# An opening written as a table of 206 steps, and attention products of 32 by 32 for the first three pieces

## The chip, the cores and the metric

The kernel runs on one core of one Trainium2 chip. The metric is device time in microseconds (us) of one execution; the median of several runs stands for a kernel. A trace was taken of one execution of the kernel before.

## The reference

A chunked state space attention (a, B, C and x of 4 batches, 8 heads, 768 steps) gives a matrix of 3072 tokens by 256. Two layers of two products each follow.

```python
# by chunks of 32 steps, per batch and head (la = log a of the chunk)
L = np.exp(cum[:, :, :, None] - cum[:, :, None, :]) * causal
M = np.einsum('bhin,bhjn->bhij', Cc, Bc) * L
y = np.einsum('bhij,bhjd->bhid', M, xc) + np.einsum('bhin,bhnd->bhid', Cc, state) * np.exp(cum)[..., None]
state = decay_full[:, :, None, None] * state + np.sum(Bx, axis=2)
...
h = x @ w_in;   x = np.maximum(0.01 * h, h) @ w_out          # first layer, 256 -> 2048 -> 256
h = np.maximum(x @ w2_in, 0.0);   out = h * h @ w2_out       # second layer
```

## The kernel before, in words

The 3072 tokens are 12 *pieces* of 256, three to a batch. For each piece the attention is made by DVE, ACT and PE, and the first layer then takes blocks of pieces: block 0 is piece 0, block 1 is piece 1, and so on, six blocks of one piece and three of two. The second layer follows by groups of 512 tokens.

*Attention of a piece.* `scan_a` squares the inputs for scales (`squares`; their sums by PE in `powers`), scales and splits every operand in a high and a low fp16 half (`him`/`kmx`, `ch`/`cl`, `xh`/`xl`), and runs two scans over the decays (`lt` and `e1`). Then PE makes S: 32 products, one for each of 16 chunks and half. As four heads lie on four strips of 32 partitions, the weights are block diagonal: `diag` puts the four strips in a cleared 128 by 128 tile (`kbd`, `xbh`, `xbl`, `sbd`), by copies on DVE and ACT for piece 0 and by DMAs for the others. S times the decays is `mk`, split in `mkh` and `mkl`. `scan_b` makes Y of 48 products, scans the states (`stt`), halves and transposes them (`shl`, `t16`), makes Z of 32 products onto Y, and writes `yh` and `yl`, the halves of the first layer's input (for piece 0 a single `y32`).

*Weights* come as 64-bit numbers, 512 KB a chunk, through seven buffers (`wst`). Each of the 16 chunks of the first layer takes two steps on ACT (`split_w`), two on DVE (`split_w1`, to `raw`), and, for the blocks from 1 on, a copy on ACT and a subtraction on DVE (`split_w2`, high and low halves). Block 0 multiplies the raw fp32 weights with `y32`; blocks from 1 on make three products for each one, of halves.

*Order.* The program is written as generators of stages that a planner (`due`, `stages_to`) draws from while blocks are written out; a scheduler then sets the order on each engine, which runs its own in that order. In block 0, `raw_step` writes the weights' steps. `sequence_scales` squares the tiles `all` of one of the later batches.

## Time and profile before

| | |
|---|---|
| median of 3 runs | 605.75 us (605.15 to 606.31) |
| the profiled execution | 606.45 us, its span 604.7 us |
| PE busy | 572.1 us, 95% |
| DVE, ACT busy | 455.6 us, 75%; 445.5 us, 74% |

The span runs from the first to the last instruction on the chip. Times in rows are from its start. An engine's busy share is a mean over stages; matmuls are pipelined, and their ends are modelled, so that one that starts 25 ns after another can be shown as 180 ns long.

### The profile page before, as it was taken

What the parts mean: (1) busy time and instruction counts of PE and PEld (TensorE: products, weight loads), DVE (VectorE), ACT (ScalarE), POOL (GpSimd) and SP (SyncE); (2) the same over time, 40 slices, a digit from 0 to 9 for tenths busy, and PEclk for the clock granted to TensorE, in tenths of its full rate; (3) what the DMA queues carried; (4) which work ended last, traced back from release to release, by engine and by line L of the source; (5) the groups of instructions that cost most, each with busy time, mean ns of one, the idle gap of its engine ahead of it and who ended that gap; (6) DMA issues with size and microseconds to landing.
All of it is one profiled execution on the core that took longest, in us unless ns stands there. A gap on an engine that the chain in (4) does not pass through costs nothing.

```text
span 604.7 us, 11654 instructions
## 1 busy us (share of the span) xinstructions
PE 572.1 (95%) x4610; PEld 516.3 (85%) x4610; DVE 455.6 (75%) x774; ACT 445.5 (74%) x715; POOL 5.2 (1%) x15
## 2 busy tenths in 40 slices
PE   0399999999999999999999999999999999999996
PEld 0388899999999878888888889989999999999996
DVE  6999989569984979567655468787777877877765
ACT  6999876479676868556665588877878777777773
POOL 3000000000000000000000000000000000000000
PEclk9999999999999999999999999999999999999999
DMA  8864845573576663131210000010000100100101
GB/s 295 289 160 129 234 111 116 129 193 92 113 187 189 163 166 36 36 62 46 69 36 0 1 2 0 2 36 1 9 28 1 35 1 2 36 1 0 36 1 35
DMA packets 113574, 46.50 MB, mean 77 GB/s; under 512 B 94448, under 2 KB 103280, under 8 KB 113520
## 3 DMA queue, kind: packets, MB, share of 16 engines
q1 hardware_dynamic: 113520, 45.76, 28.3%
q8 instruction: 36, 0.59, 0.4%
q14 instruction: 18, 0.15, 0.1%
HBM read 36.83 MB, written 3.15 MB: 66 GB/s over the span
## 4 chain that ended last, share of the span: by engine, by line
PE 86%; DVE 7%; ACT 4%; issue 2%; DMA 1%; DVEq 0%; ACTq 0%
PE hp L470 13%; PE hp L471 13%; PE hp L472 13%; PE o L532 4%; PE o L611 4%; PE o L538 4%; PE o L533 4%; PE o L609 4%; PE o L610 4%; PE oo L533 3%; PE oo L538 3%; PE oo L532 3%; PE Ym L611 3%; PE Ym L610 3%; PE Ym L609 3%
## 5 line engine op out<-in xcount | busy, mean ns | idle before, releaser
L509 DVE TENSOR_TENSOR g<-t,g 128x512 fp32r<-128x512 f32 x88 | 60.5, 687 | 52.6 <-ACT t L508 52.4
L587 DVE TENSOR_TENSOR tl<-ts,th 128x1024 fp32r<-128x1024 f32 x48 | 58.8, 1226 | 47.1 <-ACT th L585 47.1
L507 ACT ACTIVATE g<-hp 128x512 fp32r<-128x512 f32 x88 | 52.3, 594 | 47.2 <-PE o L538 33.7
L470 PE MATMUL hp<-yl,w1i 128*128 128x256 f32 (+1 forms) x256 | 83.4, 326 | 0.7 <-DVE yl L449 0.7
L471 PE MATMUL hp<-yh,w1i 128*128 128x256 f32 (+1 forms) x256 | 83.2, 325 | 0.0
L472 PE MATMUL hp<-yh,w1i 128*128 128x256 f32 (+1 forms) x256 | 83.0, 324 | 0.0
L575 ACT ACTIVATE b<-hp 128x512 f32<-128x512 f32 x96 | 57.2, 596 | 33.0 <-PE hp L472 32.8
L470 PE MATMUL hp<-xl,w2i 128*128 128x512 f32 x192 | 75.4, 393 | 0.0
L471 PE MATMUL hp<-xh,w2i 128*128 128x512 f32 x192 | 75.3, 392 | 0.0
L472 PE MATMUL hp<-xh,w2i 128*128 128x512 f32 x192 | 74.8, 389 | 0.0
L585 ACT CAST th<-ts 128x1024 fp32r<-128x1024 f32 x48 | 50.3, 1047 | 16.8 <-DVE ts L584 16.8
L470 PEld LDWEIGHTS hp<-yl,w1i 128*128 128x128 f32 x256 | 48.7, 190 | 4.9 <-DVE yl L449 1.1
L508 ACT ACTIVATE t<-hp 128x512 f32<-128x512 f32 x88 | 52.2, 593 | 0.0
L472 PEld LDWEIGHTS hp<-yh,w1i 128*128 128x128 f32 x256 | 48.7, 190 | 3.7
L471 PEld LDWEIGHTS hp<-yh,w1i 128*128 128x128 f32 x256 | 48.7, 190 | 3.7
L576 ACT ACTIVATE b<-b 128x1024 f32<-128x1024 f32 x48 | 50.9, 1061 | 1.1
L586 DVE TENSOR_TENSOR bl<-b,bh 128x768 fp32r<-128x768 f32 x48 | 45.7, 952 | 0.0
L582 DVE TENSOR_TENSOR ts<-b 128x512 f32<-128x512 f32 x48 | 33.2, 691 | 14.5 <-ACT b L576 13.5
L472 PEld LDWEIGHTS hp<-xh,w2i 128*128 128x128 f32 x192 | 36.1, 188 | 7.8
L470 PEld LDWEIGHTS hp<-xl,w2i 128*128 128x128 f32 x192 | 36.2, 189 | 6.3
L471 PEld LDWEIGHTS hp<-xh,w2i 128*128 128x128 f32 x192 | 36.2, 189 | 5.8
L581 ACT CAST bh<-b 128x768 fp32r<-128x768 f32 x48 | 40.1, 835 | 1.3
(167 smaller groups left out, 1571.4 us busy)
## 6 DMA issues: line engine op xcount, KB each, us to landing
in<-in SPq DMA_DIRECT2D x12, 640.0 KB, 4.9
in<-in SPq DMA_DIRECT2D x12, 512.0 KB, 5.7
all<-in SPq DMA_DIRECT2D x15, 384.0 KB, 4.3
wst<-w1i SPq DMA_DIRECT2D x8, 512.0 KB, 6.6
wst<-w1o SPq DMA_DIRECT2D x8, 512.0 KB, 6.4
wst<-w2i SPq DMA_DIRECT2D x8, 512.0 KB, 7.4
wst<-w2o SPq DMA_DIRECT2D x8, 512.0 KB, 4.2
out_t<-r SPq DMA_DIRECT2D x24, 128.0 KB, 1.7
```

Source lines behind the costliest of these rows:

```text
L470: nc.tensor.matmul(hp, wh[:, k, c], xl[:, :, k], start=(k == 0), stop=False)
L471: nc.tensor.matmul(hp, wh[:, k, c], xh[:, :, k], start=False, stop=False)
L472: nc.tensor.matmul(hp, wl[:, k, c], xh[:, :, k], start=False, stop=(k == KI - 1))
L507: nc.scalar.activation(g[:, 0], hp, AF.Lrelu)
L508: nc.scalar.activation(t, hp, AF.Lrelu)
L509: nc.vector.tensor_tensor(g[:, 1], t, g[:, 0].bitcast(F32), ALU.subtract)
L532: nc.tensor.matmul(self.o[d], wl[:, c], gh, start=(m == 0 and (d == 0 or self.n == 2)), stop=False, **kw)
L575: nc.scalar.activation(b[:, 2 * i : 2 * i + 2], hp.rearrange("p (n t) -> p n t", n=2), AF.Relu)
L576: nc.scalar.activation(b, b, AF.Square)
L585: nc.scalar.copy(th, t)
L586: nc.vector.tensor_tensor(bl, b[:, 1:], bh.bitcast(F32), ALU.subtract)
L587: nc.vector.tensor_tensor(tl, t, th.bitcast(F32), ALU.subtract)
```

## The change

The opening (attention of pieces 0 and 1, first steps of the 16 first-layer chunks, all of block 0 and the high halves for block 1) is no longer drawn by the planner. `ORDER` lists its steps by name, and all queues keep that order (`keep`); the low halves (`f0` to `f15`) end it. The names: `ld` a piece's loads, `l`, `a`, `r`, `e`, `f` a weight chunk's load, ACT steps, DVE steps, high and low half; `in`, `ac`, `ou` a pair of block 0's products in, activation and products out; `c0.` and `c1.` steps of the two pieces. Piece 0's first tile is loaded in two parts. Pieces 0, 1 and 2 make S, Y and Z straight from the strips, by four products of 32 by 32 weights each in place of one of 128 by 128, with no block-diagonal tiles. The planner begins with piece 2, all of whose stages now come behind the opening. Sequence scales of batch 1 are drawn one stage later, ahead of piece 3's `scan_a`.

```diff
+c0.Sl c0.u c0.rb c0.er c0.mt c0.ss a2 c0.kk c0.x3 c0.mk c0.e1 c0.xh c0.mkh c0.xl c0.dec c0.mkl
+c0.Ya a3 c0.ect c0.Yb c0.is c0.qh c0.fa r0 c0.d1 a4 c0.st l7 c0.ql c0.sh a5 c0.sl c0.tr a6 r1
...
+    def keep(ins):
+        if pinned[0]:
+            tc.keep_in_program_order(ins)
+            latest[ins.ins.engine] = ins.ins
+        return ins
...
-    def load_piece(p):
+    def load_piece(p, issue=True):
         v = sp.tile([P, U * (N + T + D)], F32, tag="in1", name="in1", bufs=2)
         w = sp.tile([P, U * 2 * T], F32, tag="in2", name="in2", bufs=2)
-        nc.sync.dma_start(v, in1[p])
-        nc.sync.dma_start(w, in2[p])
+        if issue:
+            keep(nc.sync.dma_start(v, in1[p]))
+            keep(nc.sync.dma_start(w, in2[p]))
+        else:
+            c = U * (N + T)
+            loads[p] = {
+                "b": lambda: keep(nc.sync.dma_start(v[:, :c], in1[p][:, :c]) if p == 0 else nc.sync.dma_start(v, in1[p])),
+                "w": lambda: keep(nc.sync.dma_start(w, in2[p])),
+                "x": lambda: keep(nc.sync.dma_start(v[:, c:], in1[p][:, c:])),
+            }
         return part(v, N + T, D), part(v, 0, N), part(w, T, T), part(v, N, T), part(w, 0, T), part(w, 0, T + N)
...
     def diag(p, dst, src):
+        if p == 2:
+            return src
         for h in range(4):
-            d, v = dst[quad[h], :, h, :], src[quad[h]]
-            if p > 0:
-                nc.sync.dma_start(d, v)
+            nc.sync.dma_start(dst[quad[h], :, h, :], src[quad[h]])
+        return dst
+
+    def product(o, w, m, u, **kw):
+        if len(w.shape) == 4:
+            nc.tensor.matmul(o, w[:, u], m, **kw)
+            return
+        for q in quad:
+            nc.tensor.matmul(o[q], w[q, u], m[q], **kw)
...
+    def opening_piece(p, tiles):
...
+        def M(o, w, m, **kw):
+            for h in quad:
+                keep(nc.tensor.matmul(o[h], w[h], m[h], skip_group_check=True, **kw))
...
+        def s_part(c, first):
+            if first:
+                q["S"] = pz.tile([P, U, T], F32, tag="S", name="S")
+            for u in range(U):
+                M(q["S"][:, u], q["kmx"][:, u], q[c][:, u], start=first and u == 0, stop=not first)
+
+        f["Sh"] = lambda: s_part("ch", True)
+        f["Sl"] = lambda: s_part("cl", False)
...
+        def y_part(*pairs):
+            first = "Y" not in q
+            if first:
+                q["Y"] = pz.tile([P, U, 64], F32, tag="Y", name="Y")
+            for i, (w, m) in enumerate(pairs):
+                for u in range(U):
+                    M(q["Y"][:, u, 0 : T + N], q[w][:, u], q[m][:, u], start=first and i == 0 and u % NC == 0, stop=False)
+
+        f["Ya"] = lambda: y_part(("xh", "mkh"), ("xl", "mkh"))
+        f["Yb"] = lambda: y_part(("xh", "mkl"))
...
+        def z():
+            for m in ("qh", "ql"):
+                for u in range(U):
+                    M(q["Y"][:, u, 0:T], q["t16"][:, u], q[m][:, u], start=False, stop=m == "ql")
...
 
-    loaded = {0: load_piece(0)}
-    for _ in range(W_AHEAD):
-        load_w()
...
     def stage(k):
         a = scan_a(k, loaded.pop(k)) if k < NP else iter(())
-        b = scan_b(k - 1, piece_y(k - 1)) if k > 0 else iter(())
-        bd = sequence_scales(k // NPC + 1) if k % NPC == NPC - 1 and k + 1 < NP else iter(())
+        b = scan_b(k - 1, piece_y(k - 1)) if k > 2 else iter(())
+        at = NPC if k == NPC else 2 * NPC - 1
+        bd = sequence_scales((k + NPC - 1) // NPC) if k > 2 and k % NPC == at % NPC and k + 1 < NP else iter(())
         if k <= APART:
...
             yield
 
-    sc_it = (k for k in range(NP + 1) for _ in stage(k))
-    now = [0, 0]
...
             k = next(sc_it, NP + 1)
             now[:] = (k, now[1] + 1) if k == now[0] else (k, 0)
 
-    stages_to(1)
...
+    def opening():
+        f = {}
+        for p in range(2):
+            f.update({f"c{p}.{n}": v for n, v in opening_piece(p, loaded.pop(p)).items()})
+            f.update({f"ld{p}{n}": v for n, v in loads[p].items()})
+        f["ld2"] = lambda: loaded.update({2: load_piece(2)})
+        for c in range(16):
+            f[f"l{c}"] = load_w
+            f[f"a{c}"] = split_w
+            f[f"r{c}"] = split_w1
+            f[f"e{c}"] = lambda: lows.append(split_w2())
+            f[f"f{c}"] = lambda: lows.pop(0)()
+        for c in range(KO // 2):
+            f[f"in{c}"] = lambda c=c: first.hmm([2 * c, 2 * c + 1])
+            f[f"ac{c}"] = lambda c=c: first.act([2 * c, 2 * c + 1])
+            f[f"ou{c}"] = lambda c=c: products_out(c)
+        pinned[0] = True
+        for n in ORDER:
+            f[n]()
+        while lows:
+            lows.pop(0)()
+        pinned[0] = False
+
+    opening()
+    behind = ExitStack()
+    for ins in latest.values():
```

On PE, where block 0 begins (L439/L440 and the L388 rows are Z of piece 0, `hp` and `oo` block 0's products in and out), before:

```order
L440 LDWEIGHTS sbd
L440 MATMUL Y<-ql,sbd 128x32
L493 MATMUL hp<-y_109,raw 128x256 x12
L526 MATMUL oo<-g_432,raw 128x256 x4
L493 MATMUL hp<-y_109,raw 128x256 x4
L526 MATMUL oo<-g_574,raw 128x256
```

and now:

```order
L388 LDWEIGHTS t_548
L388 MATMUL Y<-ql,t_548 32x32
L714 MATMUL hp<-y_109,raw 128x256 x4
L409 MATMUL S<-mx,ones 128x2
L714 MATMUL hp<-y_109,raw 128x256 x4
L747 MATMUL oo<-g_731,raw 128x256 x4
L714 MATMUL hp<-y_109,raw 128x256 x4
L747 MATMUL oo<-g_758,raw 128x256 x4
L714 MATMUL hp<-y_109,raw 128x256 x4
```

The 128 by 128 weight `sbd` is gone, the strips of the transposed states `t` are loaded instead, and in and out products alternate from the start; piece 1's small products stand among them in groups of 64.

On DVE, from piece 1's `yl` on before (L175 is a low half of a first-layer weight, L413 `ql`, L225 to L227 the clip of piece 3):

```order
L449 SCALAR_TENSOR_TENSOR yl<-Y,fac,yh 128x512
L175 TENSOR_TENSOR w1o<-raw,w1o 128x512
L175 TENSOR_TENSOR w1i<-raw,w1i 128x512
L413 SCALAR_TENSOR_TENSOR ql<-le,sc,qh 128x512
L175 TENSOR_TENSOR w1o<-raw,w1o 128x512
L225 TENSOR_SCALAR d1e<-in_692 128x16
L226 TENSOR_SCALAR in_692<-in_692 128x16x31
L227 MEMSET in_692 128x16
L175 TENSOR_TENSOR w1i<-raw,w1i 128x512
L509 TENSOR_TENSOR g<-t,g 128x512
L175 TENSOR_TENSOR w1o<-raw,w1o 128x512
L175 TENSOR_TENSOR w1i<-raw,w1i 128x512
```

and now, from the last low halves behind that `yl` (L349 to L356 scales of piece 2, L242 to L244 its clip, L247 and L252 its scans):

```order
L197 TENSOR_TENSOR w1o<-raw,w1o 128x512 x3
L768 COPY yf<-oo 128x256
L730 TENSOR_TENSOR g<-t,g 128x512
L349 TENSOR_SCALAR eb<-S 128x3
L242 TENSOR_SCALAR d1e<-in_807 128x16
L243 TENSOR_SCALAR in_807<-in_807 128x16x31
L350 TENSOR_SCALAR eb<-eb 128x3
L244 MEMSET in_807 128x16
L730 TENSOR_TENSOR g<-t,g 128x512
L353 TENSOR_SCALAR sc<-eb 128x3
L354 TENSOR_SCALAR isc<-eb 128x3
L247 SCALAR_TENSOR_TENSOR le<-in_807,delta 128x512
```

Before, the scales, clip and scans of piece 2 stood ahead of piece 1's `yl`, under block 0; now they stand behind it and behind all low halves. Between the `yl` of piece 1 and that of piece 2 there were 45 rows and are 74.

On PE, where block 2 begins (the first row with a new `yl`; S is piece 3's in both, Y piece 3's), before:

```order
L389 LDWEIGHTS kbd_92
L389 MATMUL S_1036<-ch_979,kbd_92 128x32
L390 LDWEIGHTS kbd_92
L390 MATMUL S_1036<-cl_1013,kbd_92 128x32
L470 MATMUL hp_1502<-yl_975,w1i_723 128x256
L471 MATMUL hp_1502<-yh_974,w1i_723 128x256
```

and now:

```order
L370 MATMUL Y_2212<-mkh_2083,xbh_90 128x48
L370 LDWEIGHTS xbh_90
L370 MATMUL Y_2212<-mkl_2084,xbh_90 128x48
L370 LDWEIGHTS xbl_91
L370 MATMUL Y_2212<-mkh_2083,xbl_91 128x48
L689 MATMUL hp_2474<-yl_1977,w1i_711 128x256
L690 MATMUL hp_2474<-yh_1976,w1i_711 128x256
```

Before, S of piece 3 stood ahead of block 2's first product; now S and all of Y of piece 3 do. On ACT, 13 squares of `all` tiles stand ahead of piece 2's `yh`, where there were seven.

## Rows read from the trace of the kernel before

**Rows 1.** The page: busy time, share and instructions of each engine.

```profile
PE 572.1 (95%) x4610; PEld 516.3 (85%) x4610; DVE 455.6 (75%) x774; ACT 445.5 (74%) x715; POOL 5.2 (1%) x15
```

**Rows 2.** Four stretches: length, busy (count) by engine, granted clock, DMA share.

```profile
0.00:29.50 29.50, 5.22 (x116) 4.85 (x116) 24.34 (x69) 23.60 (x48) 5.21 (x15) 1.00 0.82 293
29.50:63.30 33.80, 32.20 (x232) 27.29 (x232) 32.42 (x65) 31.19 (x61) 0.00 (x0) 1.00 0.57 169
63.30:91.60 28.30, 28.29 (x337) 27.76 (x338) 25.01 (x50) 22.07 (x43) 0.00 (x0) 1.00 0.61 145
91.60:604.70 513.10, 506.42 (x3932) 456.38 (x3927) 373.79 (x592) 368.66 (x565) 0.00 (x0) 1.00 0.22 55
```

**Rows 3.** What PE waited for: us in total, times, longest.

```profile
PE S L389 <- ACT kbd L355: 7.6, 1, 7.6
...
PE Y L439 <- DVE er L294: 5.2, 1, 5.2
...
PE o L532 <- DVE yf L547: 1.3, 1, 1.3
```

**Rows 4.** Timeline, start and us: `yl` of pieces 1 and 2, first products behind them.

```profile
62.51 0.75 DVE L449 SCALAR_TENSOR_TENSOR yl<-Y,fac,yh 128x512 fp32r<-128x512 f32 x1
...
63.31 0.39 PE L470 MATMUL hp<-yl,w1i 128*128 128x256 f32 x1 [0.71 <-DVE yl L449]
...
89.92 0.74 DVE L449 SCALAR_TENSOR_TENSOR yl<-Y,fac,yh 128x512 fp32r<-128x512 f32 x1
...
91.63 0.36 PE L470 MATMUL hp<-yl,w1i 128*128 128x256 f32 x1
```

**Rows 5.** Groups by line to 63.3 us; four tiles, two copies each per engine.

```profile
L355 DVE COPY kbd<-kmx 32x512 f16<-32x512 f16 x2 | 0.6, 282 | 0.0
...
L355 ACT COPY kbd<-kmx 32x512 f16<-32x512 f16 x2 | 1.2, 610 | 0.0
```

**Rows 6.** Timeline of PE: first of piece 1's 32 S products, what follows.

```profile
41.45 0.18 PE L389 MATMUL S<-ch,kbd 128*128 128x32 f16 x1
...
42.25 1.54 PE L526 MATMUL oo<-g,raw 128*128 128x256 f32 x6
```

**Rows 7.** Timeline: ACT's and DVE's first instructions on loaded data.

```profile
4.79 0.42 ACT L274 ACTIVATE sq<-in 128x256 bf16<-128x256 f32 x1 [2.57 <-DMA in<-in]
...
6.18 0.19 DVE L225 TENSOR_SCALAR d1e<-in 128x16 f32<-128x16 f32 x1 [2.58 <-DMA in<-in]
```

**Rows 8.** Timeline of DVE: low half `mkl`, a scan, steps on weights.

```profile
45.03 0.95 DVE L410 TENSOR_TENSOR mkl<-in,mkh 128x768 f16<-128x768 f32 x1
...
46.04 1.22 DVE L230 TENSOR_TENSOR_SCAN le<-in,delta 128x512 f32<-128x512 f32 x1
...
58.81 0.70 DVE L175 TENSOR_TENSOR w1i<-raw,w1i 128x512 fp32r<-128x512 f32 x1
59.42 0.70 DVE L143 SCALAR_TENSOR_TENSOR wst<-wst 128x512 int32<-128x512 int32 x1
```

**Rows 9.** Timeline of PE in block 0: first products, later groups, the last.

```profile
29.52 8.21 PE L493 MATMUL hp<-y,raw 128*128 128x256 f32 x24 [1.16 <-ACT y L444]
...
50.51 1.89 PE L526 MATMUL oo<-g,raw 128*128 128x256 f32 x8
52.23 1.89 PE L493 MATMUL hp<-y,raw 128*128 128x256 f32 x8
...
66.70 1.89 PE L526 MATMUL oo<-g,raw 128*128 128x256 f32 x8
```

**Rows 10.** Timeline of DVE: piece 2's first half, first and last of 23 instructions.

```profile
43.71 0.18 DVE L225 TENSOR_SCALAR d1e<-in 128x16 f32<-128x16 f32 x1
...
56.01 0.48 DVE L394 SCALAR_TENSOR_TENSOR in<-in,sc,le 128x256 f32<-128x256 f32 x1
```

**Rows 11.** ACT's squares to 92 us: ns min/median/max, first and last start.

```profile
L274 ACT ACTIVATE sq<-all x7: 827/838/847, 53.9 to 86.1; 128x768 bf16<-128x768 f32 x7
```

More of the change, by code (lines that the diff above doesn't have):

```diff
@@ L122, in load_w @@
             src = w_dram[nm][:, c :: KO // 2, :]
-        nc.sync.dma_start(st, src)
+        keep(nc.sync.dma_start(st, src))
         w_loaded.append((nm, c, st))
@@ L388, in scan_a @@
         for u in range(U):
-            nc.tensor.matmul(S[:, u], kbd[:, u], ch[:, u], start=True, stop=False)
-            nc.tensor.matmul(S[:, u], kbd[:, u], cl[:, u], start=False, stop=True)
+            product(S[:, u], kb, ch[:, u], u, start=True, stop=False)
+            product(S[:, u], kb, cl[:, u], u, start=False, stop=True)
         nc.vector.tensor_tensor(e1, ct_t, e1, ALU.mult)
@@ L396, in scan_a @@
         )
-        diag(p, xbl, xl)
+        xs.append(diag(p, xbl, xl))
         yield
         nc.vector.scalar_tensor_tensor(mk[:, :, :T], S, kk, lt, ALU.mult, ALU.mult)
-        parts[p] = ch, e1, mk, mkh, mkl
+        parts[p] = ch, e1, mk, mkh, mkl, *xs
     def scan_b(p, get_y):
         _, _, scc, _, fac, kk, rr = scales[p]
-        ch, e1, mk, mkh, mkl = parts.pop(p)
+        ch, e1, mk, mkh, mkl, xh, xl = parts.pop(p)
         nc.scalar.copy(mkh, mk)
@@ L417, in scan_b @@
             o = Y[:, u, 0 : T + N]
-            nc.tensor.matmul(o, xbh[:, u], mkh[:, u], start=(u % NC == 0), stop=False, skip_group_check=True)
-            nc.tensor.matmul(o, xbh[:, u], mkl[:, u], start=False, stop=False, skip_group_check=True)
-            nc.tensor.matmul(o, xbl[:, u], mkh[:, u], start=False, stop=False, skip_group_check=True)
+            product(o, xh, mkh[:, u], u, start=(u % NC == 0), stop=False, skip_group_check=True)
+            product(o, xh, mkl[:, u], u, start=False, stop=False, skip_group_check=True)
+            product(o, xl, mkh[:, u], u, start=False, stop=False, skip_group_check=True)
         yield
@@ L492, in hmm @@
                     for k in range(KI):
-                        nc.tensor.matmul(to, w[:, k, c], y32[:, k], start=(k == 0), stop=(k == KI - 1))
+                        keep(nc.tensor.matmul(to, w[:, k, c], y32[:, k], start=(k == 0), stop=(k == KI - 1)))
                 else:
@@ L525, in omm @@
                         w = w_raw["1o", m // 2][:, m % 2, d * P : d * P + P]
-                        nc.tensor.matmul(self.o[d], w, g, start=(m == d == 0), stop=(m == KO - 1), **kw)
+                        keep(nc.tensor.matmul(self.o[d], w, g, start=(m == d == 0), stop=(m == KO - 1), **kw))
                 return
@@ L653, in stage, with products_out @@
             yield
-    sc_it = (k for k in range(NP + 1) for _ in stage(k))
-    now = [0, 0]
+    sc_it = (k for k in range(2, NP + 1) for _ in stage(k))
+    now = [1, 1000]
     cum = []
     def stages_to(x):
-        while now[0] < NP + 1 and now[0] + min(now[1] / (2 * NSTEP if now[0] <= APART else NSTEP), 0.99) < x:
+        while now[0] < NP + 1 and now[0] + min(now[1] / (2 * NSTEP if 2 < now[0] <= APART else NSTEP), 0.99) < x:
             k = next(sc_it, NP + 1)
             now[:] = (k, now[1] + 1) if k == now[0] else (k, 0)
-    stages_to(1)
-    stages_to(1.5)
-    for _ in range(PRE):
-        raw_step()
+    first = One(0, 1)
+    lows = []
+    def products_out(c):
+        first.omm([2 * c, 2 * c + 1])
+    def opening():
[23 more added lines that the diff above has]
+    for ins in latest.values():
+        behind.enter_context(tc.issue_after(ins))
+    first.finish()
     todo = []
@@ L701, in ssd_moe_kernel @@
     for i, ms in todo:
+        if i == 0:
+            pos += 2
+            continue
+        if i == 2 and ms[0] == 0:
+            behind.close()
         p0, n = blocks[i]
@@ L706, in ssd_moe_kernel @@
         ph_ = ones_[i]
-        (need_raw if i == 0 else need)("1i", m // 2)
+        need("1i", m // 2)
         ph_.hmm(ms)
```

261 lines of the change are left out of this document (196 added, 65 removed).

## The prediction, made before the changed kernel was run

> **What bounds the kernel now.** I read the engines' line of the page first, then four stretches side by side, then what PE waited for, then the places where the stretches meet. PE is busy 572.1 of 604.7 us [rows 1]. So whatever does not make products cheaper can win at most PE's idle time, 32.6 us. The stretches say where that lies [rows 2]: 29.5 − 5.2 = 24.3 us before block 0 starts, 1.6 us under block 0, nothing from 63.3 to 91.6 us (28.29 of 28.30 busy), and 6.7 us in all the rest. The longest single waits are those of piece 0's products S and Z, 7.6 and 5.2 us [rows 3], and both are within the work that the change rewrites.
>
> The same rows show a second thing, which decides more. Up to 91.6 us DVE is busy 24.3 + 32.4 + 25.0 = 81.8 us and ACT 23.6 + 31.2 + 22.1 = 76.9 us [rows 2]. Both are almost full from their first data on. PE's first product of block 1 follows DVE's low half of piece 1's y: it starts at 62.51, the product at 63.31 after a wait on just that. The same pair for piece 2 stands at 89.92 and 91.63 [rows 4]. From 91.63 on PE runs almost unbroken to the end. So I work out one moment, X, the start of block 2's first product, and what PE has left to do then; the time moves with X.
>
> The profiled execution took 606.45 us around its span of 604.7, so 1.75 us lie outside. It is 0.7 us above the median, 605.75. I work out X against 91.63 of the profiled span and put the difference on the median.
>
> **The change, part by part.** *Diagonal copies of piece 0.* Eight on DVE at 0.28 us and eight on ACT at 0.61 [rows 5] go: 2.2 and 4.9 us of busy time, all in the first 29.5 us. For pieces 1 and 2 it is DMAs that go; nothing in the sum depends on these.
>
> *Products of 32 by 32.* Each of the 112 products of a piece (32 of S, 48 of Y, 32 of Z) becomes four, 448 in all, with a weight load each. No row shows one. The nearest is the product with a 128 by 128 weight: the 32 of piece 1's S start at 41.45, the next product at 42.25 [rows 6], so 25 ns each with its load. The four small ones of a group stand on four different strips of rows and of columns and together move what the one moved. If they run side by side, a piece costs 112 × 0.025 = 2.8 us as before; if each takes a slot as the big one did, 448 × 0.025 = 11.2 us. I take the lower end, since it is the same data through the same array.
>
> Here the notes speak on both sides. The Trainium skill's page "TensorEngine Tiling (Array Packing)", Instruction Overhead, speaks against this change: each matmul carries some 60 cycles of overhead, and one should not take a tiling factor out of a dimension that is already small. By that rule 32 columns by 32 weights gain nothing, and the second rival's time below holds. The Trainium skill's "TensorE: Matmul & The Clock Gate", Part 3, has matmuls on different row groups start some 4 ns apart; by that the sum is the forecast's. No row here can decide between them.
>
> *Piece 0's chain, to T0 (PE starts block 0).* The first tile now comes in two parts, with a and the transposed B between them. DVE's first data came at 6.18 us, ACT's at 4.79 [rows 7], so 512 KB took 1.39 us; with 256 KB moved behind, DVE starts at 5.5. Then in DVE's new order: clip 0.5, scales 0.6, scan 1.1, kmx and cl 0.7 each with a wait for ACT's high parts: 9.4. S's scale steps and the tail columns 1.3, mk 0.7: 11.4. ACT has three weight chunks and xh ahead of mkh, so mkh ends at 13.0; mkl 0.95 [rows 8]: 14.1; the rest of Y 0.9; d1s after qh: 15.9; a weight chunk's two steps and the state scan: 16.8; the states' halves and the transpose, between ACT's chunk 4: 18.9; Z and y 1.7. T0 = 20.6, where it was 29.5 [rows 9].
>
> *From T0 to block 1, DVE.* Fourteen weight chunks of two steps at 0.6 us (58.81 to 59.42 in [rows 8]): 16.9. Piece 1: two scans 2.3, eight operations near 0.66, mkl 0.9, clip, tail columns and the small half 1.5, eighteen small ones 1.8: 11.7. Five low halves of weights 3.0; y's half and yl 1.1. Sum 32.7, and with some 0.3 us of waits yl of piece 1 ends at 53.2, not 63.2.
>
> *The same stretch, PE.* Block 0's 128 records at 1.72 us for eight [rows 9]: 27.5. Its first 24 records took 8.0 us where three times 1.72 is 5.2, a slow start of 2.8, though the granted clock reads 1.00 there [rows 2]; I keep that. Piece 1's products 2.8, sums of scales 0.6. 33.7 us: PE is through with block 0 at 54.3. Before, it began block 1 at 63.3 and still had eight records at 66.70, 1.7 us [rows 9], so the opening is 10.7 us ahead on PE.
>
> *What block 1 gives back.* The first half of piece 2's attention ran on DVE from 43.71 to 56.01 us, under block 0 [rows 10]. Now it comes after the low halves, as the order's rows show. Two scans 2.3, kmx, cl, xl 2.0, C times decay 0.6, tail columns and clip 0.9, thirteen small ones 0.9: 6.7 us. DVE was busy 25.0 us from 63.3 to 91.6. To this come the 6.7, piece 3's mk 0.7 and five steps on second-layer weights 3.0, which now stand ahead of piece 2's yl, less one g 0.6: 34.8; added up row by row at start-to-start steps I get 33.8, and use 34. ACT: 22.1, plus piece 2's squares and scalings 4.3, plus six more squares of the sequence tiles (13 stand ahead of piece 2's yh, seven did) at 0.84 us [rows 11] 5.0, plus 3.3 for second-layer weights, less 2.6 for first-layer ones that are earlier now: 32.1. PE has 160 products of 0.12 us, 19, and 4 us of attention: 23.
>
> So DVE and ACT lead PE here. Piece 2's yl ends at 53.2 + 34 = 87.2; with both engines nearly full and waiting for each other I add 1.0 (bounds 0 and 2): 88.2. Block 2's first product also stands behind piece 3's Y: DVE's cl and mkl 1.6, then 48 products 1.2. **X = 91.0**, against 91.63: 0.6 earlier. By then 12 products more are left of block 1 than before (1.4) but Y of piece 3 is done (1.2): 0.2 later. Sum −0.4: **605.3 us**. Of the 10.7 us that PE is ahead at block 1, some 10 are lost waiting in block 1.
>
> *At nothing:* the finer loads (a weight buffer comes free seven chunks ahead, some 14 us, the load is hidden in that), the order kept by queues, finish() of block 0 ahead of block 1. Without that cover a chunk's load of 1.4 us would stand in DVE's lane.
>
> *Bounds of the sum.* Without any idle time DVE has 13.5 us of piece 0 with two chunks, 32.7 and 33.8 from 5.5 us on: 85.5 for yl, X = 88.3, **602.6 us**. Were the 32.1 us of ACT and 34 of DVE to add waits of 2 us rather than 1, 606.3.
>
> **The rivals.** *Slower: the small products go one by one* (place: S, Y, Z of pieces 0 to 2). At 25 ns each, T0 is 8.4 later, 29.0. Block 0 on PE takes 27.5 + 2.8 + 11.2 + 0.6 = 42.1: to 71.1; piece 1's Z ends two groups of eight records (3.4) before that, yh and yl 1.5 after: 69.2. DVE's 34 and 1.0: 104.2, then 2.8: X = 107.0, 15.4 later, **621 us**. It speaks for it that 25 ns has been the least spacing for 32 and 48 columns alike [rows 6].
>
> *Slower by a little: two pairs in the time of one,* 12.5 ns: T0 21.5, block 0 through at 58.3, yl 56.4 because Y of piece 1 comes late to the state scan, X = 93.3: **608 us**. From about 11 ns the change is measurably slower; above that each ns costs some 1 us.
>
> *Faster: the waits of DVE and ACT all but vanish,* the order fits: 602.6, and the 1.3 us wait for yf at a later block [rows 3] goes as well: 601.3 to 603.6, say **603**. Against it: five places in DVE's new order wait for a result of ACT or PE in the walk above.
>
> *PE keeps its 10 us:* that asks that DVE do 34 us of block 1's work in 25, and I give it 1 in 100.
>
> **How the numbers follow.** A difference under 0.2%, 1.2 us, is about what a measurement of this kernel can't tell from none. Forecast (603.6 to 606.9 as its own range): 0.42. Pairs at 10 to 20 ns, 606.9 to 613: 0.22. One by one, 613 to 621: 0.18. Waits vanish, faster: 0.18. Of the forecast's range 0.13 lies below 604.5, 0.25 within, 0.04 above. Faster 0.31, same 0.26, slower 0.43. The range leaves out the one-by-one case and little else: 602 to 614.
>
> **What would show it.** Right: block 0 starts near 20.6 us, block 1 near 54; DVE and ACT both over 95% busy from there to piece 2's yl near 88; PE waits some 8 us inside block 1, on piece 2's transposed state and yl; 448 small products in near 2.8 us; block 2 near 91. Wrong: small products 25 ns apart and PE never idle in block 1 (second time above), or block 2 well before 88 us.

## The result, and the profile after

The changed kernel takes 612.58 us (median of 4 runs, 610.96 to 614.44), beside 606.03 us of the kernel before on the same chip: ratio 1.011, 95% interval 1.007 to 1.015. It is slower, inside the forecast's range but 7.3 us above the forecast. The profiled execution took 614.08 us around a span of 612.3.

Three lines of the changed kernel's page: PE's busy time, the granted clock in forty slices, the queue that fetches instructions.

```profile
PE 580.1 (95%) x5622; PEld 522.4 (85%) x5622; DVE 458.3 (75%) x774; ACT 442.8 (72%) x707; POOL 5.4 (1%) x15
...
PEclk9999978999999999999999999999999999999999
...
q8 instruction: 44, 0.72, 0.5%
```

Against [rows 1] this is the first thing to see: PE's idle time is what it was (612.3 − 580.1 = 32.2 us, 32.6 before), and its busy time is 8.0 us more. The stretches, cut at block 0's start, block 1's start and X (columns as in [rows 2]), say where both lie:

```profile
0.00:25.59 25.59, 6.21 (x453) 5.47 (x453) 18.42 (x43) 16.93 (x34) 5.43 (x15) 1.00 0.72 258
25.59:62.25 36.66, 35.16 (x580) 29.68 (x581) 34.88 (x71) 32.68 (x63) 0.00 (x0) 1.00 0.78 256
62.25:100.30 38.05, 32.54 (x705) 30.95 (x703) 35.76 (x80) 34.25 (x70) 0.00 (x0) 0.87 0.56 150
100.30:612.30 512.00, 506.23 (x3895) 456.25 (x3890) 369.22 (x584) 358.93 (x542) 0.00 (x0) 1.00 0.20 47
```

The opening has 19.4 us of idle PE, 4.9 less than before [rows 2]; block 1 now has 5.5 us where there was none. X is 100.30, not 91.63, so from there on the kernel runs as before (512.0 us to the end, 513.1 before). DVE and ACT are busy 35.8 and 34.3 of 38.05 us in block 1: the give-back is there. What the forecast does not have is in the clock column, cut here at the times at which the clock changes:

```profile
76.88:83.70 6.82, 6.77 (x162) 6.28 (x166) 4.94 (x12) 3.81 (x8) 0.00 (x0) 0.50 0.85 290
83.70:93.95 10.25, 6.53 (x251) 6.13 (x237) 10.22 (x22) 10.25 (x21) 0.00 (x0) 1.00 0.26 34
93.95:97.36 3.41, 3.41 (x49) 3.37 (x38) 3.03 (x5) 3.41 (x7) 0.00 (x0) 0.50 0.30 36
```

For 10.2 us PE runs at the lower level, 1.2 GHz; the kernel before had no such stretch behind its start. In the first one ACT, which was ahead, waited 3.0 us for PE, as its timeline says:

```profile
82.48 0.60 ACT L728 ACTIVATE g<-hp 128x512 fp32r<-128x512 f32 x1 [3.01 <-PE hp L691]
```

PE's waits, columns as in [rows 3]:

```profile
PE S L409 <- ACT sq L291: 8.1, 2, 5.4
PE Y L388 <- issue: 3.7, 4, 2.5
PE Y L388 <- DVE t L381: 3.6, 1, 3.6
PE Y L388 <- ACT mkh L513: 2.8, 1, 2.8
PE S L370 <- ACT wst L155: 1.6, 1, 1.6
...
PE Y L373 <- issue: 1.2, 1, 1.2
...
PE S L373 <- issue: 0.9, 1, 0.9
```

"Issue" is a wait for nothing that the profile names; below it is called a stop. It stands only at lines 388 and 373, the 32 by 32 products, 5.8 us in all. PE's timeline in piece 0's S and Y shows their pace and the longest such stop:

```profile
10.12 0.69 PE L388 MATMUL S<-ch,kmx 32*32 32x32 f16 x64 [0.88 <-DVE eb L381]
...
14.50 0.83 PE L388 MATMUL Y<-mkh,xh 32*32 32x48 f16 x64 [2.83 <-ACT mkh L513]
15.12 0.48 PE L388 MATMUL Y<-mkh,xl 32*32 32x48 f16 x26
18.08 0.58 PE L388 MATMUL Y<-mkh,xl 32*32 32x48 f16 x38 [2.49 <-issue]
```

From 14.50 to 15.12 there are 64 products of 48 columns, 9.7 ns each. In S (32 columns) 64 take 0.69 us, of which 0.18 is the length of the last one: 8.1 ns. The forecast took 6.3 (25 ns for four).

### The profile page after: what moved, and what is told of

It reads as the page before. It is cut to its first block, busy times and chain, and to the rows that moved or that the text cites. A ratio compares the mean times of both kernels' runs of the same rounds, so it can differ in the third digit from the quotient of the medians.

```text
span 612.3 us, 13621 instructions
## 1 busy us (share of the span) xinstructions
PE 580.1 (95%) x5622; PEld 522.4 (85%) x5622; DVE 458.3 (75%) x774; ACT 442.8 (72%) x707; POOL 5.4 (1%) x15
## 4 chain that ended last, share of the span: by engine, by line
PE 86%; DVE 7%; ACT 3%; issue 2%; DMA 1%; SPq 0%; DVEq 0%; ACTq 0%
PE hp L690 13%; PE hp L689 13%; PE hp L691 13%; PE o L753 4%; PE o L832 4%; PE o L759 4%; PE o L754 4%; PE o L830 4%; PE o L831 4%; PE Y L370 3%; PE oo L753 3%; PE oo L759 3%; PE oo L754 3%; PE Ym L832 3%; PE Ym L831 3%; PE Ym L830 3%
## 5 line engine op out<-in xcount | busy, mean ns | idle before, releaser
L728 ACT ACTIVATE g<-hp 128x512 fp32r<-128x512 f32 x88 | 52.3, 595 | 50.7 <-PE o L759 34.5
L690 PE MATMUL hp<-yh,w1i 128*128 128x256 f32 (+1 forms) x256 | 84.2, 329 | 0.0
L691 PE MATMUL hp<-yh,w1i 128*128 128x256 f32 (+1 forms) x256 | 83.9, 328 | 0.0
L690 PEld LDWEIGHTS hp<-yh,w1i 128*128 128x128 f32 x256 | 49.8, 195 | 3.7
L691 PEld LDWEIGHTS hp<-yh,w1i 128*128 128x128 f32 x256 | 49.7, 194 | 3.7
L753 PE MATMUL oo<-g,w1o 128*128 128x256 f32 x160 | 41.7, 292 | 0.0
## 6 DMA issues: line engine op xcount, KB each, us to landing
in<-in SPq DMA_DIRECT2D x12, 512.0 KB, 5.0
wst<-w1i SPq DMA_DIRECT2D x8, 512.0 KB, 7.4
wst<-w1o SPq DMA_DIRECT2D x8, 512.0 KB, 4.9
wst<-w2i SPq DMA_DIRECT2D x8, 512.0 KB, 5.9
wst<-w2o SPq DMA_DIRECT2D x8, 512.0 KB, 4.2
```

The lines of the kernel that those rows point to most:

```text
L690: nc.tensor.matmul(hp, wh[:, k, c], xh[:, :, k], start=False, stop=False)
L691: nc.tensor.matmul(hp, wl[:, k, c], xh[:, :, k], start=False, stop=(k == KI - 1))
L728: nc.scalar.activation(g[:, 0], hp, AF.Lrelu)
L753: nc.tensor.matmul(self.o[d], wl[:, c], gh, start=(m == 0 and (d == 0 or self.n == 2)), stop=False, **kw)
```

## The experiments

Fourteen kernels, each beside runs of the kernel before. Block starts are counted in the records (96 products of the first half to a block of one piece); "half" is the time at the lower clock, without the run-out at the end. These columns and PE's busy time come from one profiled execution, which took 614.50 us in squares_later, 626.21 in table_128 and 605.21 in wide_squares_later, and lies within 1.6 us of the median in the others. A *lane* is the row of work that one engine has to get through. The theories: **A**, DVE's and ACT's lanes set the end; **A2**, those lanes up to piece 3's `yl`; **P**, the small products cost PE; **C**, the clock; **F**, PE runs out of fetched instructions; **Q**, the gain lies in piece 0's chain.

| kernel | median us | ratio to before (95%) | block 0 | block 2 (X) | block 3 | half us | PE busy |
|---|---|---|---|---|---|---|---|
| before | 606.03 | 1 | 29.5 | 91.6 | 119.5 | 0 | 572.1 |
| changed | 612.58 | 1.011 (1.007 to 1.015) | 25.6 | 100.3 | 127.9 | 10.2 | 580.1 |
| x_behind | 613.98 | 1.0129 (1.0107 to 1.0151) | 24.2 | 101.5 | 129.1 | 10.2 | 580.4 |
| pairs_apart | 612.81 | 1.0116 (1.0093 to 1.0138) | 23.4 | 100.0 | 127.5 | 10.2 | 580.5 |
| squares_later | 618.32 | 1.0201 (1.0158 to 1.0243) | 23.2 | 91.4 | 128.7 | 6.8 | 579.6 |
| squares_later_128 | 622.07 | 1.0266 (1.025 to 1.0282) | 23.0 | 97.2 | 136.5 | 17.1 | 580.8 |
| squares_middle | 615.62 | 1.0148 (1.0133 to 1.0164) | 23.7 | 94.3 | 126.7 | 13.7 | 581.5 |
| products_alone | 621.81 | 1.0249 (1.0233 to 1.0266) | 34.8 | 105.7 | 134.2 | 3.4 | 577.9 |
| table_128 | 623.25 | 1.0285 (1.0258 to 1.0312) | 25.0 | 106.6 | 134.7 | 20.5 | 581.1 |
| pad_90 | 649.79 | 1.0713 (1.0695 to 1.0731) | 60.0 | 135.9 | 163.5 | 10.2 | 619.6 |
| wide_no_copies | 609.78 | 1.0061 (1.0043 to 1.0079) | 22.5 | 85.1 | 119.2 | 6.8 | 575.4 |
| s_five_times | 620.45 | 1.0243 (1.0222 to 1.0265) | 23.1 | 106.3 | 133.9 | 13.7 | 582.7 |
| filled | 622.32 | 1.0262 (1.0237 to 1.0287) | 23.4 | 108.9 | 137.5 | 20.5 | 596.0 |
| piece0_alone | 611.48 | 1.009 (1.0075 to 1.0105) | 35.2 | 94.4 | 122.7 | 3.4 | 573.7 |
| table_piece0 | 608.30 | 1.0037 (1.0024 to 1.0049) | 23.7 | 93.5 | 121.6 | 6.8 | 577.0 |
| wide_squares_later | 608.50 | 1.0035 (1.0014 to 1.0055) | 21.8 | 87.3 | 118.2 | 3.4 | 574.1 |

**x_behind** moves the squares of piece 0's x (`sqx`) behind `him` and `ch` in the table; `sfx` and `l5` go behind `ch` with them.

```diff
-ld0b ld0w ld0x l0 l1 c0.d0 l2 c0.sqb ld1b c0.sqc l3 c0.clip c0.sf ld1w c0.sqx c0.b1 c0.b2 l4
-c0.b3 c0.b5 c0.lt c0.him c0.sfx l5 c0.ch l6 c0.kmx a0 c0.x1 c0.x2 c0.cl c0.Sh a1 c0.x4 c0.b4
+ld0b ld0w ld0x l0 l1 c0.d0 l2 c0.sqb ld1b c0.sqc l3 c0.clip c0.sf ld1w c0.b1 c0.b2 l4
+c0.b3 c0.b5 c0.lt c0.him c0.ch c0.sqx c0.sfx l5 l6 c0.kmx a0 c0.x1 c0.x2 c0.cl c0.Sh a1 c0.x4 c0.b4
```

> The changed kernel with one step of its table moved: the squares of piece 0's x stand behind the two scalings him and ch on ACT, not ahead of them. In the changed kernel these squares waited until 7.88 us for their part of the load, and him, ch and so kmx and S stood behind them. Theory A (DVE's and ACT's lane from the first data on sets the end; each us that piece 0's chain is late comes back whole): block 0 starts at 24.3 instead of 25.6, block 2's first product at 99.0 instead of 100.3, 611.3 us. Rival F (the 2.5 us in the middle of piece 0's Y, in which PE waited for nothing that the profile names, end when an instruction packet lands and not when PE gets there): the gap still ends near 18.1, block 0 starts at 25.2 to 25.6 and the time stays within 0.4 of 612.6.

Block 0 did start at 24.2, but the edit cannot be credited with it: with these squares where they were, pairs_apart, both squares_later kernels, squares_middle, s_five_times, filled and table_piece0 start it at 23.0 to 23.7 and table_128 at 25.0. The arrival of x and the stop inside piece 0's Y (1.81 us here, 2.49 in the changed kernel) differ from execution to execution. Block 1 began 3.2 us later than in the changed kernel: there was a stop of 2.65 us inside piece 1's Y, then 3.4 us at half clock from 54.1 us on. A was wrong on the time.

**pairs_apart** puts the second of the two DVE steps of a raw weight behind the next step of the table on DVE.

```diff
+            if ins.ins.engine == mybir.EngineType.DVE:
+                flush()
...
-            keep(nc.vector.scalar_tensor_tensor(w.bitcast(I32), w1, -(1 << 31), w0, ALU.bitwise_and, ALU.bitwise_or))
+            later.append(
+                lambda: keep(
+                    nc.vector.scalar_tensor_tensor(w.bitcast(I32), w1, -(1 << 31), w0, ALU.bitwise_and, ALU.bitwise_or)
+                )
+            )
```

> The changed kernel, with the second of the two steps on DVE that make a raw weight put behind the next DVE step of the table, so that it no longer follows the step that it reads from. Theory A: back to back a pair took 1.32 us where two independent steps of this size take 1.21; 14 pairs stand between block 0's start and piece 1's yl, so yl of piece 1 ends 1.5 us earlier (59.0 instead of 60.5) and block 2 starts at 98.8; 611.1 us. Rival (the 0.1 us is the pipeline of DVE, which the other neighbours pay as well): the same sum of steps, under 0.4 us gained.

Nothing was gained, as the rival had it. Piece 1's `yl` ended at 59.9 us, 36.5 us behind block 0's start, where the changed kernel took 34.9.

**squares_later** and **squares_later_128**

```diff
+        if p == 2:
+            behind_y.extend((y1.ins, y2.ins))
...
-            squares(mx[:, to : to + 1], t)
+            held(squares, mx[:, to : to + 1], t)
```

with `held` queueing what it writes behind those two instructions; the second kernel also drops the lines `if p == 2: return src` of `diag`, and queues the later weight steps (`split_w2`, `w_one`) behind the same instructions. So it differs from the first in two things, where its expectation names one.

> The changed kernel, with the squares of all later batches (sequence tiles) queued behind piece 2's yh on ACT, so that piece 3's and 4's scalings and the second layer's weight steps come behind piece 2's y too. DVE then has some 8 us less between piece 1's yl and piece 2's yl, ACT some 14 us less. Theory A (DVE's and ACT's lane inside block 1 sets block 2's start): piece 2's yl ends at 60.5 + 28 = 88.5 instead of 96.4, block 2 starts at 92 to 93 instead of 100.3, and the time falls to 605 to 607, less what piece 3 gives back at block 3. Rival C (PE itself sets it: the 32 by 32 products of piece 2 with their gaps, and the two stretches in which its clock was granted at half): yl of piece 2 stays above 94, and the half-clock stretches stay with about the same length; 611 to 612.

> squares_later with one more edit: piece 2 has its block diagonal weights of 128 by 128 again (by DMA). Rival C: no stretch of half clock in block 1 any more and no gap inside piece 2's products; block 2 starts 3 us or more earlier than in squares_later, and the time is 3 us lower. Theory A: PE's waits are those of DVE and ACT, the clock falls in them whichever shape the products have, and block 2 starts within 1.5 us of squares_later's (three diagonal DMAs of some 2 us each come into piece 2's chain).

X fell by 8.9 us, to 91.4, as A had it, and nothing was won: the profiled execution took 614.50 us, the changed kernel's 614.08, and the other three of squares_later were longer (617.4 to 620.7), for a reason that no trace here shows. Three stretches of squares_later (start to block 1, to X, to block 3; columns as above):

```profile
0.00:60.46 60.46, 41.59 (x1032) 35.39 (x1033) 53.20 (x113) 48.90 (x95) 5.43 (x15) 1.00 0.77 265
60.46:91.44 30.98, 27.19 (x621) 26.08 (x619) 24.82 (x57) 18.64 (x35) 0.00 (x0) 0.94 0.20 65
91.44:128.72 37.28, 33.61 (x446) 32.97 (x445) 30.95 (x54) 29.13 (x59) 0.00 (x0) 0.97 0.58 128
```

ACT and DVE have the work of piece 3 still to do; its `yl` ends at 125.8, and block 3 starts at 128.7, 0.8 later than in the changed kernel. The waits went one block on. With 128 by 128 weights in piece 2 the transfers of its diagonals put waits of up to 3.3 us in, and half clock rose to 17.1 us. C had expected no half clock in block 1, and the clock fell there at 93.6 us, behind such a wait and with no small product near: the fall does not need them. As this kernel has new waits and a second edit, it does not tell what small products do by themselves, nor what its 3.8 us more are made of.

**squares_middle** holds the second batch's squares behind `d1s` instead (the same edit with another instruction).

> The changed kernel with the squares of the second batch queued behind piece 2's d1s on ACT and those of the later two behind piece 2's yh; squares_later had all of them behind yh, and block 2 then started at 91.4 but piece 3's yl only ended at 125.8, so that block 3 started at 128.7, later than the changed kernel's 127.9. Theory A2 (what counts is the later of two lanes: PE's from block 2's start and DVE's and ACT's up to piece 3's yl): block 2 at 92 to 94, piece 3's yl at 118 to 122, block 3 at 121 to 124 and the time 606 to 609. Rival (PE's half clock and packet stops keep block 2 late): block 2 after 97, block 3 after 126, 611 or more.

X came at 94.3, nearly A2's, but `yl` of piece 3 only at 124.5 and block 3 at 126.7: the time is the rival's, for a reason that is neither's.

**products_alone** is the kernel before with

```diff
+        if p < 3:
+            return src
...
+        for q in quad:
+            nc.tensor.matmul(o[q], w[q, u], m[q], **{**kw, "skip_group_check": True})
```

> The kernel before with one part of the change alone: the products of the attention of pieces 0, 1 and 2 are 32 by 32, without diagonal copies; no table, the planner as before. Theory P (the small products are what costs: 10 ns each, stops of PE for instruction packets inside their runs, and a clock granted at half behind them): PE needs some 2 us more a piece, one or more stretches of half clock of 3.4 us or more appear between 35 and 100 us where before had none, and the time is 1 to 3 us longer: 607 to 609. Theory A (DVE's and ACT's lane): 2.2 us of copies on DVE and 4.9 on ACT go from the opening, PE has room, the clock stays full as before: 604.5 to 606.

The direction is P's, but the kernel is 15.3 us longer than the kernel before beside it (606.54), where at most 3 were expected. Not all of it is price: the scheduler now put piece 1's S ahead of piece 0's Z, and block 0 starts 5.2 us later. PE's records in which "issue" ended a wait before block 1:

```profile
26.95 0.20 PE L362 MATMUL S<-ch,kmx 32*32 32x32 f16 x2 [1.42 <-issue]
...
33.15 0.21 PE L362 MATMUL Y<-qh,t 32*32 32x32 f16 x2 [1.37 <-issue]
...
42.53 0.20 PE L362 MATMUL Y<-mkh,xl 32*32 32x48 f16 x2 [1.74 <-issue]
...
54.84 0.19 PE L362 MATMUL S<-ch,kmx 32*32 32x32 f16 x4 [1.64 <-issue]
```

Counted in PE's records from the start, they stand at products 350, 478, 734 and 990: 128, 256 and 256 apart. A product is two instructions (weight and product). A packet of the instruction queue is 0.72 MB by 44, 16 KB, and the changed kernel's 5622 products took 44 packets, the 4610 of the kernel before 36: 128 products to a packet. So the stops stand one or two packets apart.

**table_128** keeps the table and gives pieces 1 and 2 their block diagonal weights back.

```diff
-            for h in quad:
-                keep(nc.tensor.matmul(o[h], w[h], m[h], skip_group_check=True, **kw))
+            if len(w.shape) == 3:
+                keep(nc.tensor.matmul(o, w, m, skip_group_check=True, **kw))
```

> The changed kernel with its table, but pieces 1 and 2 have products with block diagonal weights of 128 by 128 again (copied by DMA); piece 0 keeps 32 by 32. Theory P: from block 0's start to its last product PE takes 32 to 33.5 us instead of 36.6, with no half-clock stretch before block 1; piece 1's yl ends 3 us earlier than in the changed kernel relative to block 0's start; 609 or less in all. Theory A: DVE's 35 us from block 0's start to piece 1's yl stay (34.5 to 35.5), block 2 starts within 1 us of the changed kernel's, 611.5 to 613, plus what the diagonal DMAs add.

Both theories missed. Piece 0's part is as in the changed kernel, but the order is pinned and each diagonal takes 2.0 to 2.6 us from issue to landing; PE waited for them (`sbd` 3.4 and 2.7 us, `xbl` 2.1, `mkh` behind `kbd` 3.2), and half clock doubled. The kernel tells what DMA costs in this table, not what the small products do.

**pad_90**

```diff
+                for _ in range(90 if p == 0 else 0):
+                    keep(nc.tensor.matmul(q["Sf"][:, 0:1], ones, pm, start=True, stop=True, skip_group_check=True))
```

> The changed kernel with 90 more small products of a matrix of ones ahead of the first sums of piece 0, where PE waits; their result is overwritten. In four runs of the table PE stopped for nothing named always at its products 222 and 859, 1.0 to 2.5 us, each time as an instruction packet was under way. Theory F (PE runs out of fetched instructions, at a fixed count of them): the stops stand again at 222 and 859 by count, which is now the pause between piece 0's S and Y, and no stop is left inside Y of piece 0; block 0 starts 1 to 2.4 us earlier, and the later stops move 90 products too. Rival (the stop belongs to these products, a bank of PSUM or the loads of weights beside them): the stop stays inside Y of piece 0, now at product 312.

A pad in fp32 is two records and took some 0.38 us, so the whole kernel moved by 34 us: its time tells nothing. The place of the stop does. It left its old place in Y, between the 26th and 27th product with `xl`, and stood 77 products further, at record 479, which is 222 + 257, twice 128 and one. F's count of 222 was wrong, but the stop follows the count and not the products; the rival falls. The other traces agree: 37 stops stand in twelve kernels, all at a count (from zero) that is 88 to 95 above a multiple of 128, and each ends 1.2 to 1.6 us after a packet of the instruction queue has ended.

**wide_no_copies**

```diff
-            for h in quad:
-                keep(nc.tensor.matmul(o[h], w[h], m[h], skip_group_check=True, **kw))
+            keep(nc.tensor.matmul(o, w, m, skip_group_check=True, **kw))
+
+        def weight(n, u):
+            return q[n].rearrange(fl)[:, u // 4 * P : u // 4 * P + P]
```

> The changed kernel with one 128 by 128 product in place of each four of 32 by 32 in pieces 0 to 2, its weight read straight from the tile of four chunks (kmx, xh, xl, t16) with no diagonal copies. This leaves out the part of the computation that separates the heads, so the values of y are others; every load, every step of DVE and ACT and the table stay. It is the table with products at their old price. Theory P (the small products cost PE: 10 ns each in place of 6.3, stops for instruction packets, half clock): PE's busy time falls by 6 to 8 us, no packet stop is left in the first 100 us, at most one stretch of half clock; the time is 603.5 to 607, near the forecast of 605.3. Theory A2 (DVE's and ACT's lanes up to piece 3's yl): the time stays at 610 or more.

It takes 609.78 us: 2.8 us less than the changed kernel, 3.7 more than before. The first figure is rough, since the shortest execution of the changed kernel took 610.96 us and the longest of this one 610.72. No stop by "issue" is left, and PE is busy 4.7 us less. The time lies between the two theories' ranges. Its stretches (to block 0, block 1, X, block 3, block 4):

```profile
0.00:22.47 22.47, 5.46 (x117) 4.99 (x117) 18.41 (x43) 17.11 (x34) 5.40 (x15) 1.00 0.82 292
22.47:56.98 34.51, 33.26 (x245) 28.34 (x245) 33.59 (x69) 32.16 (x63) 0.00 (x0) 1.00 0.82 271
56.98:85.07 28.09, 24.12 (x273) 23.30 (x271) 27.63 (x69) 25.93 (x54) 0.00 (x0) 0.94 0.64 190
85.07:119.19 34.12, 32.37 (x438) 31.60 (x437) 32.74 (x55) 26.21 (x50) 0.00 (x0) 1.00 0.50 102
119.19:146.27 27.08, 27.08 (x338) 26.91 (x337) 20.86 (x40) 17.13 (x31) 0.00 (x0) 1.00 0.47 93
```

X is 6.6 us earlier than before the change, and block 3 starts where it did (119.19, 119.53). The opening's 7.3 us of saved idle time came back: 4.0 in block 1 (3.3 of it one wait for ACT's `t`, the clock at half behind it) and 1.8 in block 2, and more near the end (a wait for `yf`, 2.4).

**s_five_times**

```diff
+            for _ in range(5 if p == 1 and first else 1):
```

> The changed kernel with the first half of piece 1's S made five times over (256 more products of 32 by 32 in the table, where block 0 runs; the last one counts). Theory P: 256 times 10 ns is 2.6 us, with two more instruction packets that stop PE up to 1 to 2.5 us each; block 0's last product 2.6 to 6 us later and the time 2 to 6 us longer: 614.5 to 618.5. Theory A2 (DVE's lane is full there and PE has slack): under 1 us later, 612 to 613.5.

It takes 7.9 us more than the changed kernel, above P's range. PE's timeline there:

```profile
38.76 1.95 PE L388 MATMUL S<-ch,kmx 32*32 32x32 f16 x220
46.05 0.99 PE L388 MATMUL S<-ch,kmx 32*32 32x32 f16 x100 [5.34 <-issue]
```

There are 320 products in one run: the first 220 at 8.1 ns, then 5.3 us of nothing. Inside that stop, at 42.76 us, the clock fell, for 6.8 us. The instruction packet ahead of the restart began only at 43.69 us; why so late, nothing here shows. The stop, not the price, is the larger part.

**filled**

```diff
+    def fill(p, o, m, a, u):
+        if p == 2:
+            nc.tensor.matmul(o[:, a : u + 1, 0:T], zero, m[:, a : u + 1], start=False, stop=False, skip_group_check=True)
```

> The changed kernel with 48 products of a cleared 128 by 128 weight between the small products of piece 2, one behind each chunk of S, Y and Z, over up to 512 columns; they add zeros. They cost PE some 3 to 4 us in a place where it waits 5.5 us. Theory C (the clock falls to half because the engine does little during small products and the waits beside them, and that is a good part of the loss): the half-clock stretches between 62 and 98 us go or shrink from 10.2 us to 3.4 or none, block 2 starts 1 to 3 us earlier, 609.5 to 612. Rival (the waits themselves bring the clock down, or it costs nothing): the stretches stay at 6.8 us or more, block 2 at 100 or later, 612 to 616.

In this kernel the zeros also replaced some of piece 2's sums, so its values are others. It takes 9.7 us more than the changed kernel, and half clock doubled. Its rows around two falls of the clock in block 1:

```profile
62.86:73.27 10.41, 10.41 (x86) 10.18 (x84) 10.41 (x27) 10.38 (x24) 0.00 (x0) 1.00 0.71 221
73.89:76.20 2.31, 2.31 (x71) 1.59 (x71) 2.31 (x11) 2.06 (x6) 0.00 (x0) 1.00 0.39 142
76.20:83.03 6.83, 6.83 (x90) 3.90 (x82) 3.26 (x7) 4.26 (x9) 0.00 (x0) 0.50 0.94 319
83.03:89.86 6.83, 6.83 (x178) 5.33 (x177) 6.25 (x15) 5.15 (x12) 0.00 (x0) 1.00 0.29 95
89.86:96.68 6.82, 6.82 (x83) 5.94 (x76) 6.33 (x14) 5.86 (x12) 0.00 (x0) 0.50 0.67 154
```

PE has one listed wait, of 0.6 us, in all this time, none from 73.89 on, and loses its clock twice all the same. So C's remedy is wrong, and a listed wait is not needed for the fall. That PE was fully at work is not shown: ends are modelled, and where 32 by 32 products and the zero products take turns, 0.1 us or more often passes between two starts. Nor does the run separate the small products from the zero weights and from the changes between the two shapes.

**piece0_alone** is products_alone with `if p == 0` in place of `if p < 3`.

> The kernel before with 32 by 32 products for piece 0 alone, whose sixteen diagonal copies on DVE and ACT go; no table, the planner as before. Theory P: the small products cost only where PE has no idle time; in the opening it has 24 us, so DVE saves 2.2 us and ACT 4.9 of lane: block 0 starts 1 to 3 us earlier than 29.5 and the time is 603 to 605.5. Rival (the copies were beside the path, and the scheduler draws other work ahead into their place): block 0 at 29 to 32 and 605.5 to 608.

It is slower than either had it. Without the copies the scheduler drew piece 1's steps ahead, as the rival said, PE waited 8.6 us for piece 0's transposed state, and block 0 started at 35.2. So the run gives no price for the copies alone.

**table_piece0** has the changed kernel's table cut behind `c0.ya`, without the steps of piece 1 and block 0.

> The kernel before with the table for piece 0 alone: its steps, its 32 by 32 products, the first nine weight loads and the steps of the first weights in the order that the changed kernel has for them, all other work of before queued behind it; from block 0 on the planner and the block diagonal weights of pieces 1 and 2 as before. Theory Q (the gain of the change lies in piece 0's chain; what it loses is PE's: 32 by 32 products and half clock in pieces 1 and 2, and DVE's and ACT's order behind the table): block 0 starts at 23 to 25.6 instead of 29.5, the clock is full from some 29 us on, block 2 starts 3 to 5 us earlier than 91.6, the time is 601 to 604. Theory A2 (the time is set by DVE's and ACT's lanes up to piece 3's y, and what the opening wins is lost again wherever it comes from): block 2 within 2 us of 91.6, 605 to 608.

Block 0 started at 23.7, as Q expected, and the rest came as A2 had it, at the upper end: X at 93.5, 608.3 us. PE waited in the middle of block 0 for ACT's `g`, which the scheduler had put behind weight steps, and its clock fell. The timeline, then the stretches:

```profile
43.38 1.22 PE L762 MATMUL oo<-g,raw 128*128 128x256 f32 x2 [4.18 <-ACT g L737]
```

```profile
38.00:42.73 4.73, 1.19 (x6) 0.71 (x4) 4.73 (x10) 4.73 (x10) 0.00 (x0) 1.00 0.31 36
42.73:49.56 6.83, 6.18 (x45) 5.10 (x46) 4.19 (x10) 4.48 (x9) 0.00 (x0) 0.50 0.59 119
```

The wait of 4.2 us and the 3.4 us that half clock takes from PE's work in 6.8 us are more than the 5.8 us that the opening had won.

**wide_squares_later** is wide_no_copies with the squares of the third and fourth batch held as in squares_later.

> wide_no_copies (one 128 by 128 product for each four, no separation of the heads, so the values of y are others) with the squares of the third and fourth batch queued behind piece 2's yh on ACT; in wide_no_copies PE waited 3.3 us at 80 us for ACT's t, behind 11 squares, and its clock then stood at half for 3.4 us. Theory A2 (with the products at their old price the opening's gain is lost to ACT's lane in block 1 and to the clock that falls in that wait): the wait goes, PE is idle 4 us or less between block 0's start and block 4 instead of 7.0, 605 to 607.5. Rival (the lanes are full whichever way the squares stand): the same idle time at another place, 609 to 611.

The time lies between the two: 608.5 us (605.2 to 610.2). In the profiled execution, the shortest of ten, the 3.3 us wait went, one of 1.9 came elsewhere, and PE was idle 6.3 us between block 0's start and block 4, not 4. That ACT's order is some of what the table loses is not shown: the gain of 1.3 us is within the spread. The ten executions fall in two groups, five of 605.2 to 607.5 us with mean clocks of 0.994 to 0.997, and five of 609.5 to 610.2 us with 0.989 to 0.993. No version beat the kernel before.

## Why the prediction was wrong

Two steps failed: the sum had small products at the old price and with nothing behind them, and it took the clock as full throughout, so that a wait of PE cost its own length and no more. The runs showed 4.0 us a piece and stops, and 4.9 to 8.6 us of lost clock in each execution.

*The price of small products: wrong, and the sum's first failed step.* "Side by side", 2.8 us a piece or 6.3 ns each, was taken as nearest to the rows; they took 8.1 in S, 8.6 in Z (64 in 0.72 us, reckoned alike) and 9.7 in Y. With 128, 128 and 192 of them a piece costs 4.0 us, not 2.8. The rival at 12.5 ns had the kind right, though its T0 of 21.5 does not follow: 5.6 us a piece in place of 2.8 would make it 23.4. Its threshold (measurably slower from 11 ns on) was wrong, since the price was not all. The Trainium skill's "TensorE: Matmul & The Clock Gate", Part 3, has starts some 4 ns apart, and "TensorEngine Tiling (Array Packing)", Instruction Overhead, some 60 cycles a product, an estimated 25 ns at 2.4 GHz; the measured 8 to 10 ns lie between. At 25 ns the one-by-one rival, 621 us, would hold, which the prediction there calls the second.

*Stops for instructions: in no part of the prediction.* They take 5.8 us in the profile, and none is left with wide products. That they come from instruction fetch rests on their counts, one packet's worth of products or a multiple of it apart, and on the packet that ends 1.2 to 1.6 us ahead of the end of each of the 37 (from 15.52 to 16.64 us for the stop that ends at 18.08). The trace names no releaser, but pad_90 leaves no room for the products themselves. The Trainium skill's "Runtime: NRT & Kernel Launch", Instruction fetch mechanics, has blocks of 256 instructions, which agrees with 128 products, and their fetch mostly hidden, which does not agree with stops of up to 5.3 us.

*The clock: in no part either, and the largest loss.* I forecast 8 us of PE's waits in block 1 (5.5 measured) and priced them as waits alone. Four executions of the changed kernel have spans of 612.3, 612.7, 609.3 and 609.2 us with mean clocks of 0.989, 0.986, 0.992 and 0.992 (before: 0.998): the same program is 3 us longer when 2 to 4 us more of clock are lost. Half of 10.2 us is 5.1 us of PE's work, the largest item of its extra busy time. Span times one minus the mean clock is the clock that an execution lost, an estimate from the recorded figures: at the median 5.8 us in the changed kernel, 5.2 in wide_no_copies, 4.2 in table_piece0, and 0.6 (0 to 2.4) in 44 executions of the kernel before. What is left of the span has the median 604.3, 602.6, 602.4 and 603.4 us. If a lost us of clock cost a us, as when PE has work all the time, 5.2 of the 6.5 us would be clock, and with wide products all of the loss.

*T0, 20.6 forecast, 25.6 measured.* Of the 5.0, 2.5 are the stop in Y, up to 1.2 are piece 0's share of the price, and some 1.5 are x's part of the load, for which ACT waited until 7.88: `him` behind it started at 8.51, and at 6.8 to 7.0 in six of the kernels with the same steps for piece 0. So part of it is this execution's own; those six start block 0 at 23.0 to 23.7, with stops of 0.8 to 1.8 us, still 2.4 us or more late.

*Block 0 on PE, 33.7 us forecast, 36.7 measured.* With products at the old price it is 34.5 (wide_no_copies), so the term was right but for price and stops. The DVE sum, 32.7 + 0.3 us to piece 1's `yl`, was 34.9; from 20.6 it gives 53.6, where the prediction has 53.2.

*The give-back: right.* 36.7 us from block 1 to X were forecast, 38.05 measured, with DVE and ACT busy 94% and 90% of it.

*"The time moves with X": wrong as a rule.* It held for the changed kernel (X 8.7 us later, span 7.6 longer). But squares_later has the X of before in an execution of 614.5 us, and wide_no_copies has an X 6.6 us earlier than before in one of 609.2 us: what is not done by X is waited for at block 3. The landmark would have to be PE's work done, over all of the first blocks.

*The account.* In the profiled executions PE is busy 8.0 us more: up to 5.1 by half clock and 3.0 to 3.6 by small products, less 1.0 in block 0. The 3.6 is 1.2 us a piece more; the 3.0 is what wide_no_copies saves, 4.7 us, less 1.7 for its 3.4 us less of half clock. In block 0 the products are busy 31.4 us, 32.4 before, as eight of them and not thirteen start at twice the later spacing. PE is idle as long as before: 4.9 us less in the opening, 5.5 more in block 1. The products' own part of the loss, with the stops and the clock that go with them, is the 2.8 us between the changed kernel and wide_no_copies, a rough figure; the other 3.7 us stay with wide products, of which its own 6.8 us at half clock make 3.4. What stays open is what brought the clock down in the changed kernel: ahead of both of its falls there are 128 small products and waits of 0.3 to 1.6 us. Waits between wide products did it with no small product near (4.2 us in table_piece0, 3.3 in wide_no_copies), and in filled it fell without a listed wait.

## What to carry to other kernels

A shorter start was worth nothing here, as the engines behind it were full; follow the freed time over several blocks and by the busy engine's work done, not by one start time. Cutting a product in four costs instructions: look at the pace, and at stops without a releaser, and count the records between them. Read the mean granted clock of every execution beside its time, and price a wait of PE with the clock that falls behind it: 4.2 us of wait cost 7.6 in table_piece0.
